# Two up/down layers behind a windowed attention: raw weights loaded in halves, on-chip places handed out by another rule, and q and k of three units loaded first

## The chip, the cores and the metric

The kernel runs on one core of a Trainium2 chip. Its time is the device time of one execution in microseconds (us); 1197.46 us is the median of three runs before the change. The engines are named as in the profile: PE (matrix products; PEld its weight loads), DVE (VectorE), ACT (ScalarE), POOL (GpSimd) and SP (SyncE, which issues all DMAs here).

## What is computed

Windowed attention over 4 batches of 768 positions with 8 heads, then two feed-forward layers over the 3072 tokens, all in float32 out (the weights come in float64):

```
# attention, per chunk of 32 queries: keys are 8 memory slots and positions -16 .. +8 around the chunk
scores = scale * q_c @ k_full.T ; a = softmax(scores) ; out = a @ v_full
x = out, heads joined: [3072, 512]
h = x @ w_in            # [512, 2048]          "up 1"
x = (s * relu(h)**2 + b) @ w_out               # "down 1"
h = x @ w2_in           # [512, 2048]          "up 2"
y = (h - tanh(h)) @ w2_out                     # "down 2"
```

## The kernel before

The program is one stream of code; PE, DVE, ACT and POOL run it in the order in which it is written, and SP issues the DMAs in one queue. Every large product is made of three matmuls on split operands (three(), L132: high by high, low by high, high by low; 128 x 384 results), so each operand is split into a high part by ACT (a copy to the matmul type) and a low part by DVE or POOL (a subtraction).

**Start and up 1** (0 to 398.4 us). Attention runs over 24 units of 128 tokens, three to a block of 384. For a unit u, scores (L192, 16 small matmuls; the masks are added by DVE into sm, L212, and the row maximum taken, L217), exps (ACT), norm (POOL multiplies, L236), transposes (PE, ACT copies into pt), values (PE) and take_x (ACT xh, DVE xl, L276). A block of up 1 has 16 tiles, called slots; a tile needs xh, xl of its three units and wh, wl of a weight pair. The eight pairs (class Pair1, L288) are made from raw float64 words in steps: a (ACT, L145), b (two DVE instructions, L148 and L149), c (DVE, L154), d (ACT, L308), e (DVE, L312); each instruction goes over 1024 columns. Three more sets of eight raw pieces (class Other, L658: w_out, the second w_in, the second w_out) are converted by the same three functions of to_f32 (L138) in the later blocks and stored to HBM. Four tiles make a quad: ob1, ob2 hold its results, POOL combines them into ot1, ot2 (combine1), and five parts are stored to HBM (o<-ob, o<-ot). An agenda of (slot, function) pairs sets when the steps of attention, conversions and loads come between the tiles (L636 to L733).

**Down 1** (to 639.5 us) and **down 2** (from 955.6 us) use a seven-product scheme (P1 to P7) on quadrants, with a ring of split operands (ringh by ACT, ringl by DVE).

**Up 2** (639.5 to 955.6 us) uses seven products as well. It goes in 32 runs, a run being one piece n of weights by one group g of 768 tokens; runs over g 0, 1 come first, those over g 2, 3 behind. In a loop step i (L984) group1(i) makes P1, P6, P5; group3(i - 1) makes P4 and P3 of the run before, adds, applies tanh, lets POOL combine (L337) and stores; group2(i) makes P2 and P7. In every other run the next weights are made by w2_make (ACT w2h, DVE w2l: L802, L803 and L810). In runs 14 to 19 both() (L480) splits x2f, the operands of g 2 and 3, which were put into HBM in down 1.

**Places.** The arena of on-chip memory is cut into places by size in columns of 4 bytes per partition: 3 H (384), 16 G (768), 28 Z (1024), 4 F (1536), 4 E (2048). take() gets one, drop() gives it back with a stamp of the drop counter. grab() (L81) takes, among G and Z that fit, the one dropped longest ago (with an exception that spares Z), else F, else E. A tile in a place can be written only when all readers and writers of the place's last tile are done; that wait lands on the engine that first writes the new tile. The raws (2048 columns) come from E, tmp (three pieces of 384 columns) from F or E, tmp2 (two pieces) from any but H.

Of the kernel before, what the change touches and what calls it, by code (L numbers as in the profile page):

```python
# [25 lines left out]
NB = 384  # L26
# [15 lines left out]
def tile_chunk_attention_two_ffn(  # L42
# [34 lines left out]
    SIZE = {"H": 384, "G": 768, "Z": 1024, "F": 1536, "E": 2048}  # L77
# [3 lines left out]
    clock = [0]  # L81

    def grab(n, only="HGZ"):
        fit = [(free[k][0][0], SIZE[k], k) for k in SIZE if k in only and n <= SIZE[k] and free[k]]
        if any(f[2] in "GZ" for f in fit):
            fit = [f for f in fit if f[2] in "GZ"]
        elif any(f[2] == "F" for f in fit):
            fit = [f for f in fit if f[2] == "F"]
        if not fit and not free["E"]:
            raise MemoryError(sorted((v[1].name.split("_")[0], v[0]) for v in held.values()))  # L90
        if not fit:
            return free["E"].pop(0)[1]
        if n <= SIZE["H"] and free["H"]:
            k = "H"
        else:
            k = min(f for f in fit if f[2] != "Z" or n > SIZE["G"] or len(free["Z"]) > 3 or len(fit) == 1)[2]
        return free[k].pop(0)[1]
# [40 lines left out]
    def to_f32(z, raw):  # L138

        pair = raw.rearrange("p (n two) -> p n two", two=2)  # L140
        lo32, hi32 = pair[:, :, 0], pair[:, :, 1]
        zi = z.bitcast(I32)

        def rebase():
            nc.scalar.activation(out=z, in_=hi32.bitcast(F32), func=AF.Copy, scale=2.0 ** -112)  # L145

        def high():
            nc.vector.tensor_single_scalar(zi, zi, 3, op=ALU.logical_shift_left)  # L148
            nc.vector.scalar_tensor_tensor(  # L149
                out=zi, in0=hi32, scalar=-(1 << 31), in1=zi, op0=ALU.bitwise_and, op1=ALU.bitwise_or  # L150
            )

        def low():
            nc.vector.scalar_tensor_tensor(  # L154
                out=zi, in0=lo32, scalar=29, in1=zi, op0=ALU.logical_shift_right, op1=ALU.bitwise_or
            )

        return rebase, high, low
# [124 lines left out]
    def load_raw(src, n):  # L283
        raw = take(2048, I32, "raw", "E")
        nc.sync.dma_start(out=raw, in_=src.bitcast(I32)[n])
        return raw

    class Pair1:  # L288
# [13 lines left out]
        def c(self):  # L302
            self.low()
            drop(self.raw)
# [182 lines left out]
    def minus(x, y, o=None):  # L487
        o = o if o is not None else take(2 * NB, F32, "t", "GZE")
        nc.gpsimd.tensor_tensor(out=o, in0=x, in1=y, op=ALU.subtract)
        return o  # L490
# [78 lines left out]
    load_qk(0)  # L569
    load_qk(1)  # L570
    load_v(0)
    pairs = [Pair1(0)]
    load_qk(2)
# [3 lines left out]
    load_qk(3)  # L577
    nc.sync.dma_start(out=s_c, in_=s.partition_broadcast(P))
    nc.sync.dma_start(out=b_c, in_=b.partition_broadcast(P))
    pairs.append(Pair1(2))  # L580
    load_v(3)
# [18 lines left out]
    scores(1, (5, 6))  # L600
    exps(0)
# [15 lines left out]
    norm(2)  # L617
    pairs[1].a()
    values(1)
    loads_to(5, 4)  # L620
    take_x(1)
    pairs[1].b()
    transposes(2)
# [3 lines left out]
    values(2)  # L627
    scores(3)
    loads_to(6, 5)
    pairs[1].e(nc.vector)  # L630
    take_x(2)
# [9 lines left out]
    v_slot = {3: 7.0, 4: 10.5, 5: 13.8}  # L641
    for u in range(6, NU):
        v_slot[u] = 16 * (u // 3 - 1) + (3.2, 8.5, 13.6)[u % 3]
    s_slot = {3: 0.0, 4: 3.5}
    for u in range(5, NU):
        s_slot[u] = v_slot[u - 2]
    for u in range(3, NU):
        s0, v0 = s_slot[u], v_slot[u]
        if u > 3:
            at(s0 + 0.001, scores, u)  # L650
        at(s0 + 1.0, exps, u)
        at(s0 + 3.2, norm, u)
        at(v0 - 2.3, transposes, u)
        at(v0, values, u)
        at(v0 + 0.002, take_x, u)
        at(v0 + 0.003, loads_to, u + 4, u + 3)

    class Other:  # L658
# [14 lines left out]
        def c(self):  # L673
            self.low()
            drop(self.raw)
# [119 lines left out]
    def w2_make(n, part):  # L795
        z = z_in[n][part]
        size = (768, 1024)[part]
        h, l = take(size, F32R, "w2h"), take(size, F32R, "w2l")
        if part == 0:
            nc.scalar.activation(out=h[:, 0:512], in_=z[:, 0:512], func=AF.Copy)  # L800
            nc.scalar.activation(out=h[:, 512:768], in_=z[:, 512:768], func=AF.Copy, scale=-1.0)
            nc.vector.tensor_tensor(out=l[:, 0:512], in0=z[:, 0:512], in1=h[:, 0:512].bitcast(F32), op=ALU.subtract)  # L802
            nc.vector.scalar_tensor_tensor(  # L803
                out=l[:, 512:768], in0=z[:, 512:768], scalar=-1.0, in1=h[:, 512:768].bitcast(F32),
                op0=ALU.mult, op1=ALU.subtract,
            )
# [115 lines left out]
    def group1(i):  # L922
        q = quad[i] = {}
        q["a"], q["b"], q["d"] = (bank(k)[:, 0:NB] for k in (i % 2, 2 + i % 3, 5 + i % 3))
        q["tmp"] = take(3 * NB, F32, "tmp", "FE"), take(2 * NB, F32, "tmp2", "GZFE")
        q["p1"], q["u2"], q["u3"] = (q["tmp"][0][:, NB * k:NB * (k + 1)] for k in range(3))
        q["r1"], q["r2"] = (q["tmp"][1][:, NB * k:NB * (k + 1)] for k in range(2))
# [6 lines left out]
    def group2(i):  # L934
# [3 lines left out]
        b1, b2 = (piece(t) for t in q["o"])  # L938
        product(i, "P2", q["a"], False, True)
        product(i, "P7", q["b"], False, True)  # L940
        nc.scalar.activation(out=q["r1"], in_=q["a"], func=AF.Tanh)
        nc.vector.tensor_tensor(out=q["u3"], in0=q["p1"], in1=q["b"], op=ALU.add)  # L942
        nc.vector.tensor_tensor(out=b2[:, 0], in0=q["u3"], in1=q["d"], op=ALU.add)  # L943
        nc.scalar.activation(out=q["r2"], in_=b2[:, 0], func=AF.Tanh)
        nc.vector.tensor_tensor(out=b1[:, 1], in0=q["a"], in1=q["r1"], op=ALU.subtract)
        nc.gpsimd.tensor_tensor(out=b2[:, 0], in0=b2[:, 0], in1=q["r2"], op=ALU.subtract)

    def group3(i):
# [15 lines left out]
        t12, t34 = (piece(t) for t in q["o"][2:])
# [18 lines left out]
    w2_load(1)  # L983
    for i in range(NR + 1):  # L984
# [111 lines left out]
```

## Time and profile before

| | us |
|---|---|
| median of three runs (lowest, highest) | 1197.46 (1196.81, 1198.2) |
| the profiled run | 1198.98 |
| its span, first to last instruction | 1197.2 |
| PE busy in the span | 1093.5 |
| DVE, ACT, POOL busy | 834.9, 569.1, 545.3 |

The profiled run is 1.5 us above the median, and its span 1.8 us below its own time. A row of waits names the line of the waiting instruction, what released it, and the total, the count and the longest of such waits. [...] A tile stands by its name without its number.

### The profile page before, as it was taken

The numbers are of one execution on the slowest core, as the hardware profiler recorded it, in microseconds if no ns is written. First come the engines' busy times: TensorE is split into PE (matmuls) and PEld (weight loads), VectorE is DVE, ScalarE is ACT, GpSimd is POOL, SyncE is SP. The second block draws the span as 40 slices with busy tenths as digits, with TensorE's granted clock in tenths as the row PEclk, the third lists the DMA queues.
The fourth block names the chain that finished last, engine by engine and source line by source line (L and its number), as shares of the span: only waits on it lengthen the run. The fifth ranks groups of instructions, "written<-read, shape, count | busy, mean of one in ns | idle before, by whom it ended". The sixth has DMA issues, their size and how long they took to land. (4 is left out here: it accounts for less than half of the span.)

```text
span 1197.2 us, 19711 instructions
## 1 busy us (share of the span) xinstructions
PE 1093.5 (91%) x7296; PEld 1062.8 (89%) x7296; DVE 834.9 (70%) x1012; ACT 569.1 (48%) x1121; POOL 545.3 (46%) x428
## 2 busy tenths in 40 slices
PE   4789999899999999999899997867897899999998
PEld 3678999899999999999899997856787789999998
DVE  5676777777763776789796776755555596777664
ACT  5455666565653554455453343332233354444442
POOL 2135456689565721324543665533454672231010
PEclk8779999999999999999999999987989899999999
DMA  9965999999988766666475667833545876668783
GB/s 282 296 226 206 351 343 347 363 352 350 349 289 323 263 199 196 195 201 197 161 251 179 239 233 278 284 136 130 194 160 197 324 247 211 187 201 248 235 240 103
DMA packets 129344, 292.28 MB, mean 244 GB/s; under 512 B 10720, under 2 KB 76256, under 8 KB 125152
## 3 DMA queue, kind: packets, MB, share of 16 engines
q1 hardware_dynamic: 129248, 291.02, 71.6%
q8 instruction: 57, 0.93, 0.3%
q14 instruction: 39, 0.32, 0.1%
HBM read 175.38 MB, written 115.61 MB: 243 GB/s over the span
## 5 line engine op out<-in xcount | busy, mean ns | idle before, releaser
L136 PE MATMUL pb<-ringl,whh 128*128 128x384 f32 x896 | 301.4, 336 | 4.1 <-DVE ringl L413 2.4
L134 PE MATMUL pb<-ringh,whh 128*128 128x384 f32 x896 | 300.5, 335 | 3.6 <-ACT ringh L407 3.6
L135 PE MATMUL pb<-ringh,whl 128*128 128x384 f32 x896 | 300.3, 335 | 0.0
L413 DVE TENSOR_TENSOR ringl<-part,ringh 128x768 fp32r<-128x768 f32 x160 | 202.2, 1283 | 79.8 <-ACT ringh L412 79.7
L412 ACT ACTIVATE ringh<-part 128x768 fp32r<-128x768 f32 x160 | 135.0, 848 | 151.7 <-PE pb L135 148.4
L134 PE MATMUL pb<-x2h,w2h 128*128 128x384 f32 x448 | 160.6, 358 | 39.3 <-DVE tmp L942 20.0
L136 PE MATMUL pb<-xl,wh 128*128 128x384 f32 x512 | 175.6, 343 | 6.6 <-DVE xl L276 6.5
L134 PE MATMUL pb<-xh,wh 128*128 128x384 f32 x512 | 179.7, 351 | 0.0
L135 PE MATMUL pb<-xh,wl 128*128 128x384 f32 x512 | 174.9, 342 | 0.0
L136 PEld LDWEIGHTS pb<-ringl,whh 128*128 128x128 f32 x896 | 168.9, 188 | 6.8 <-DVE ringl L413 3.7
L135 PE MATMUL pb<-x2h,w2l 128*128 128x384 f32 x448 | 159.1, 355 | 14.9 <-DVE w2l L810 9.9
L134 PEld LDWEIGHTS pb<-ringh,whh 128*128 128x128 f32 x896 | 169.2, 189 | 3.9 <-ACT ringh L407 3.9
L135 PEld LDWEIGHTS pb<-ringh,whl 128*128 128x128 f32 x896 | 169.0, 189 | 0.0
L136 PE MATMUL pb<-x2l,w2h 128*128 128x384 f32 x448 | 158.1, 353 | 0.0
L329 DVE SCALAR_TENSOR_TENSOR ob<-pb,r 128x384 f32<-128x384 f32 x128 | 69.8, 552 | 91.6 <-ACT r L328 86.2
L134 PEld LDWEIGHTS pb<-x2h,w2h 128*128 128x128 f32 x448 | 90.4, 202 | 47.5 <-DVE tmp L942 22.5
L328 ACT ACTIVATE r<-pb,s_c 128x384 f32<-128x384 f32 x128 | 72.4, 577 | 114.3 <-PE pb L136 108.8
L408 DVE SCALAR_TENSOR_TENSOR ringl<-part,b_c,ringh 128x768 fp32r<-128x768 f32 x64 | 92.6, 1476 | 21.7 <-ACT ringh L407 21.7
L395 POOL TENSOR_TENSOR whl<-s,whh 128x1024 fp32r<-128x1024 f32 x16 | 41.0, 2563 | 144.2 <-ACT whh L394 144.2
L136 PEld LDWEIGHTS pb<-xl,wh 128*128 128x128 f32 x512 | 98.7, 193 | 8.2 <-DVE xl L276 8.1
L135 PEld LDWEIGHTS pb<-x2h,w2l 128*128 128x128 f32 x448 | 90.4, 202 | 17.5 <-DVE w2l L810 11.4
L134 PEld LDWEIGHTS pb<-xh,wh 128*128 128x128 f32 x512 | 99.2, 194 | 2.9 <-issue 0.4
(95 smaller groups left out, 1788.9 us busy)
## 6 DMA issues: line engine op xcount, KB each, us to landing
o<-ot SPq DMA_DIRECT2D x128, 384.0 KB, 4.1
part<-o SPq DMA_DIRECT2D x112, 384.0 KB, 3.9
part<-o SPq DMA_DIRECT2D x56, 768.0 KB, 4.7
o<-ob SPq DMA_DIRECT2D x64, 384.0 KB, 4.5
raw<-in_wi_dram SPq DMA_DIRECT2D x16, 1024.0 KB, 9.3
raw<-in_wo_dram SPq DMA_DIRECT2D x16, 1024.0 KB, 8.1
o<-ob SPq DMA_DIRECT2D x64, 192.0 KB, 3.1
k<-in_qk_dram SPq DMA_DIRECT2D x24, 384.0 KB, 8.6
```

What stands on the lines that cost most here:

```text
L134: nc.tensor.matmul(acc, lhsT=whi, rhs=xhi, start=first, stop=False, skip_group_check=more)
L135: nc.tensor.matmul(acc, lhsT=wlo, rhs=xhi, start=False, stop=False, skip_group_check=more)
L136: nc.tensor.matmul(acc, lhsT=whi, rhs=xlo, start=False, stop=last, skip_group_check=more)
L328: nc.scalar.activation(out=r, in_=ps, func=AF.Identity, scale=s_c[:, 0:1])
L329: nc.vector.scalar_tensor_tensor(out=dst, in0=ps.rearrange("p (n t) -> p n t", n=2), scalar=0.0, in1=r.rearrange("p (n t) -> p n t", n=2), ...
L395: eng.tensor_tensor(out=lo, in0=src, in1=hi.bitcast(F32), op=ALU.subtract)
L408: nc.vector.scalar_tensor_tensor(out=xl, in0=src, scalar=self.bias, in1=xh.bitcast(F32), op0=ALU.add, op1=ALU.subtract)
L412: nc.scalar.activation(out=xh, in_=src, func=AF.Copy)
L413: nc.vector.tensor_tensor(out=xl, in0=src, in1=xh.bitcast(F32), op=ALU.subtract)
```

## The change

Four things are changed.

- **Raw weights in halves.** load_raw takes two tiles of 1024 columns and issues two DMAs; to_f32 goes over 512 results for each half in rebase, high's second instruction and low.
- **Places.** E is gone, its memory becomes eight more Z (36). grab goes through kinds in order: H, then G (from the beginning of up 2 on, when spare is set: the oldest of G, Z and F), then Z, then F. w2h and w2l may use F from then on.
- **tanh into the result's place.** A run of up 2 has one tmp of two pieces of 384 columns in place of tmp and tmp2 with five; each tanh and the sum u3 are written into a half of ob1 or ob2 that is still free. The tanh of P2 and its subtraction come ahead of the two adds of P7.
- **Start.** q and k of units 0, 1 and 2 are loaded first, v behind raw 0; the scores of unit 2 follow those of 1, unit 3's go into the agenda; the slots of units 3 to 5 move by -0.2 to +1.3, those of the later ones by -0.4 to -0.6.

The diff, cut to its core:

```diff
-    COUNT = {"H": 3, "G": 16, "Z": 28, "F": 4, "E": 4}
+    COUNT = {"H": 3, "G": 16, "Z": 36, "F": 4}
     def grab(n, only="HGZ"):
...
+        for kinds in ("H", "GZF" if spare[0] else "G", "Z", "F"):
+            fit = [(free[k][0][0], k) for k in kinds if k in only and n <= SIZE[k] and free[k]]
+            if fit:
+                return free[min(fit)[1]].pop(0)[1]
...
+            for o, lo32, _ in parts:
+                oi = o.bitcast(I32)
+                nc.vector.scalar_tensor_tensor(
+                    out=oi, in0=lo32, scalar=29, in1=oi, op0=ALU.logical_shift_right, op1=ALU.bitwise_or
+                )
...
-        raw = take(2048, I32, "raw", "E")
-        nc.sync.dma_start(out=raw, in_=src.bitcast(I32)[n])
+        raw = [take(1024, I32, nm) for nm in ("raw0", "raw1")]
+        for h in range(2):
+            nc.sync.dma_start(out=raw[h], in_=src.bitcast(I32)[n][:, 1024 * h:1024 * (h + 1)])
...
-        q["tmp"] = take(3 * NB, F32, "tmp", "FE"), take(2 * NB, F32, "tmp2", "GZFE")
+        q["tmp"] = take(2 * NB, F32, "tmp", "GZF")
...
         product(i, "P2", q["a"], False, True)
+        nc.scalar.activation(out=b1[:, 1], in_=q["a"], func=AF.Tanh)
         product(i, "P7", q["b"], False, True)
-        nc.scalar.activation(out=q["r1"], in_=q["a"], func=AF.Tanh)
-        nc.vector.tensor_tensor(out=q["u3"], in0=q["p1"], in1=q["b"], op=ALU.add)
-        nc.vector.tensor_tensor(out=b2[:, 0], in0=q["u3"], in1=q["d"], op=ALU.add)
-        nc.scalar.activation(out=q["r2"], in_=b2[:, 0], func=AF.Tanh)
-        nc.vector.tensor_tensor(out=b1[:, 1], in0=q["a"], in1=q["r1"], op=ALU.subtract)
-        nc.gpsimd.tensor_tensor(out=b2[:, 0], in0=b2[:, 0], in1=q["r2"], op=ALU.subtract)
+        nc.vector.tensor_tensor(out=b1[:, 1], in0=q["a"], in1=b1[:, 1], op=ALU.subtract)
+        nc.vector.tensor_tensor(out=b2[:, 1], in0=q["p1"], in1=q["b"], op=ALU.add)
+        nc.vector.tensor_tensor(out=b2[:, 0], in0=b2[:, 1], in1=q["d"], op=ALU.add)
+        nc.scalar.activation(out=b1[:, 0], in_=b2[:, 0], func=AF.Tanh)
+        nc.gpsimd.tensor_tensor(out=b2[:, 0], in0=b2[:, 0], in1=b1[:, 0], op=ALU.subtract)
...
     w2_load(1)
+    spare[0] = True
```

First place: DVE in up 2, from group2 of one run to group2 of the next, in which weights are made (the names with numbers are the tiles of the two runs). Before:

```order
L931 TENSOR_TENSOR tmp<-tmp,pb 128x384
L954 TENSOR_TENSOR pb<-tmp,pb 128x384
L957 TENSOR_TENSOR pb<-tmp,pb 128x384
L959 TENSOR_TENSOR ob_8267<-pb,tmp_8207 128x384
L960 TENSOR_TENSOR ob_8266<-pb,tmp_8207 128x384
L802 TENSOR_TENSOR w2l<-zina,w2h 128x512
L803 SCALAR_TENSOR_TENSOR w2l<-zina,w2h 128x256
L942 TENSOR_TENSOR tmp<-tmp,pb 128x384
L943 TENSOR_TENSOR ob_8347<-tmp,pb 128x384
L945 TENSOR_TENSOR ob_8346<-pb,tmp_8291 128x384
```

Now:

```order
L929 TENSOR_TENSOR tmp<-tmp,pb 128x384
L952 TENSOR_TENSOR pb<-tmp,pb 128x384
L955 TENSOR_TENSOR pb<-tmp,pb 128x384
L957 TENSOR_TENSOR ob_8407<-pb,ob_8407 128x384
L958 TENSOR_TENSOR ob_8406<-pb,ob_8406 128x384
L801 TENSOR_TENSOR w2l<-zina,w2h 128x512
L802 SCALAR_TENSOR_TENSOR w2l<-zina,w2h 128x256
L940 TENSOR_TENSOR ob_8485<-pb,ob_8485 128x384
L941 TENSOR_TENSOR ob_8486<-tmp,pb 128x384
L942 TENSOR_TENSOR ob_8486<-ob_8486,pb 128x384
```

The subtraction of tanh from P2's bank moves ahead of the two adds of P7, and no row writes a tile of its own for them.

Second place: SP's queue at the beginning of the program. Before:

```order
L183 DMA k<-in_qk_dram 128x768
L184 DMA q<-in_qk_dram 128x512
L183 DMA k<-in_qk_dram 128x768
L184 DMA q<-in_qk_dram 128x512
L188 DMA v<-in_vw_dram 96x1024
L285 DMA raw<-in_wi_dram 128x2048
L183 DMA k<-in_qk_dram 128x768
L184 DMA q<-in_qk_dram 128x512
L188 DMA v<-in_vw_dram 96x1024
L285 DMA raw<-in_wi_dram 128x2048
```

Now:

```order
L181 DMA k<-in_qk_dram 128x768
L182 DMA q<-in_qk_dram 128x512
L181 DMA k<-in_qk_dram 128x768
L182 DMA q<-in_qk_dram 128x512
L181 DMA k<-in_qk_dram 128x768
L182 DMA q<-in_qk_dram 128x512
L284 DMA raw_123<-in_wi_dram 128x1024
L284 DMA raw_124<-in_wi_dram 128x1024
L186 DMA v<-in_vw_dram 96x1024 x2
L284 DMA raw_131<-in_wi_dram 128x1024
L284 DMA raw_132<-in_wi_dram 128x1024
```

The loads of unit 2's k and q move from behind v and raw of the first pair to the third place in front, and each raw is two rows.

Third place: DVE between the first two take_x and the end of the second pair. Before:

```order
L276 TENSOR_TENSOR xl<-pb,xh 128x4x128
L312 TENSOR_TENSOR wl<-z,wh 128x1024
L234 TENSOR_SCALAR sums<-sums 128x8
L235 RECIPROCAL rs<-sums 128x8
L276 TENSOR_TENSOR xl<-pb,xh 128x4x128
L148 TENSOR_SCALAR z<-z 128x1024
L149 SCALAR_TENSOR_TENSOR z<-raw,z 128x1024
L154 SCALAR_TENSOR_TENSOR z<-raw,z 128x1024
L212 TENSOR_TENSOR sm<-pb,mask_mid 128x384 x2
L217 TENSOR_REDUCE nmx<-sm 128x8
L218 TENSOR_SCALAR nmx<-nmx 128x8
L312 TENSOR_TENSOR wl<-z,wh 128x1024
L276 TENSOR_TENSOR xl<-pb,xh 128x4x128
```

Now:

```order
L274 TENSOR_TENSOR xl<-pb,xh 128x4x128
L312 TENSOR_TENSOR wl<-z,wh 128x1024
L274 TENSOR_TENSOR xl<-pb,xh 128x4x128 x2
L142 TENSOR_SCALAR z<-z 128x1024
L145 SCALAR_TENSOR_TENSOR z<-raw_131,z 128x512
L145 SCALAR_TENSOR_TENSOR z<-raw_132,z 128x512
L152 SCALAR_TENSOR_TENSOR z<-raw_131,z 128x512
L152 SCALAR_TENSOR_TENSOR z<-raw_132,z 128x512
L312 TENSOR_TENSOR wl<-z,wh 128x1024
```

The scores of unit 3 (the mask's and the maximum's rows) are no longer among these, and the xl of unit 2 stands right behind that of unit 1, ahead of the second pair's conversion.

## Rows read from the trace of the kernel before

**Rows 1.** Windows by stage: us; busy us (count) of PE, PEld, DVE, ACT, POOL; clock; DMA; GB/s.

```profile
34.20:106.00 71.80, 55.89 (x445) 52.25 (x442) 51.81 (x72) 36.87 (x109) 22.78 (x17) 0.80 0.75 251
106.00:398.40 292.40, 287.35 (x2579) 277.56 (x2578) 206.51 (x302) 166.92 (x460) 188.32 (x163) 1.00 0.91 326
398.40:639.50 241.10, 235.77 (x1344) 234.09 (x1343) 197.19 (x157) 123.77 (x143) 97.61 (x39) 0.99 0.63 207
639.50:730.00 90.50, 87.09 (x494) 84.96 (x493) 65.07 (x107) 36.29 (x74) 54.62 (x53) 1.00 0.66 233
730.00:825.40 95.40, 69.84 (x339) 65.62 (x337) 60.88 (x89) 35.15 (x66) 45.02 (x40) 0.87 0.62 208
825.40:955.60 130.20, 104.92 (x517) 100.54 (x518) 68.75 (x119) 42.28 (x84) 69.12 (x67) 0.88 0.58 208
```

**Rows 2.** PE's waits, 825.4 to 955.6 us: line, releaser, us in total, times, longest.

```profile
PE pb L134 <- DVE tmp L942: 13.0, 6, 2.6
PE pb L134 <- DVE ob L943: 6.5, 4, 4.8
```

**Rows 3.** DVE's waits in the same stretch.

```profile
DVE w2l L802 <- POOL ot L337: 19.2, 6, 3.2
DVE ob L943 <- POOL ot L337: 15.2, 5, 3.8
DVE w2l L810 <- ACT w2h L809: 8.0, 6, 2.6
DVE ob L943 <- DMA o<-ot: 6.5, 3, 5.6
```

**Rows 4.** Timeline of DVE, 888 to 906.5 us: start, duration, instruction, [idle before, releaser].

```profile
895.95 0.56 DVE L943 TENSOR_TENSOR ob<-tmp,pb 128x384 f32<-128x384 f32 x1 [2.79 <-POOL ot L337]
...
903.35 1.46 DVE L802 TENSOR_TENSOR w2l<-zina,w2h 128x512 fp32r<-128x512 f32 x1 [3.20 <-POOL ot L337]
```

**Rows 5.** DVE's waits, 730 to 825.4 us.

```profile
DVE w2l L810 <- POOL ot L337: 4.2, 1, 4.2
DVE ob L943 <- DMA o<-ot: 4.2, 1, 4.2
DVE x2l L484 <- POOL ot L337: 4.1, 2, 3.2
...
DVE x2l L484 <- DMA o<-ot: 1.6, 1, 1.6
```

**Rows 6.** Groups of DVE instructions, 639.5 to 730 us: count, busy us, mean ns, idle before.

```profile
L802 DVE TENSOR_TENSOR w2l<-zina,w2h 128x512 fp32r<-128x512 f32 x6 | 4.2, 693 | 3.0 <-ACT w2h L800 3.0
```

**Rows 7.** DMA issues, 120 to 330 us: count, KB each, median us to landing.

```profile
o<-ot SPq DMA_DIRECT2D x39, 384.0 KB, 7.8
raw<-in_wo_dram SPq DMA_DIRECT2D x11, 1024.0 KB, 8.5
...
zo<-z SPq DMA_DIRECT2D x11, 512.0 KB, 4.4
```

**Rows 8.** PE's waits, 0 to 106 us.

```profile
PE pb L200 <- DMA q<-in_qk_dram: 11.8, 3, 5.1
PE pb L136 <- DVE xl L276: 3.1, 1, 3.1
```

**Rows 9.** Timeline of DVE, 33 to 39 us.

```profile
34.31 1.02 DVE L212 TENSOR_TENSOR sm<-pb,mask_mid 128x384 f32<-128x384 f32 x2 [3.12 <-PE pb L200]
...
36.43 1.22 DVE L312 TENSOR_TENSOR wl<-z,wh 128x1024 fp32r<-128x1024 f32 x1
37.57 0.68 DVE L276 TENSOR_TENSOR xl<-pb,xh 128x512 fp32r<-128x512 f32 x1
```

**Rows 10.** PE's waits, 106 to 398.4 us (up 1, blocks 1 to 7).

```profile
PE pb L136 <- DVE xl L276: 3.4, 2, 2.0
PE pb L259 <- ACT pt L246: 1.5, 2, 1.4
```

**Rows 11.** PE's waits, 398.4 to 639.5 us (down 1).

```profile
PE pb L134 <- ACT ringh L407: 3.6, 1, 3.6
```

More of the change, by code (lines that the diff above doesn't have):

```diff
@@ L73, in tile_chunk_attention_two_ffn @@
     ctx.enter_context(tc.manual_schedule(engines={ET.PE, ET.DVE, ET.Activation, ET.Pool}))
-    SIZE = {"H": 384, "G": 768, "Z": 1024, "F": 1536, "E": 2048}
-    COUNT = {"H": 3, "G": 16, "Z": 28, "F": 4, "E": 4}
+    SIZE = {"H": 384, "G": 768, "Z": 1024, "F": 1536}
+    COUNT = {"H": 3, "G": 16, "Z": 36, "F": 4}
     free = {k: [(0, f"{k}{i}") for i in range(n)] for k, n in COUNT.items()}
     held = {}
-    clock = [0]
+    clock, spare = [0], [False]
     def grab(n, only="HGZ"):
[L84 to L97, printed above, removed]
+        for kinds in ("H", "GZF" if spare[0] else "G", "Z", "F"):
+            fit = [(free[k][0][0], k) for k in kinds if k in only and n <= SIZE[k] and free[k]]
+            if fit:
+                return free[min(fit)[1]].pop(0)[1]
+        raise MemoryError(sorted((v[1].name.split("_")[0], v[0]) for v in held.values()))
     def put_back(place):
@@ L303, in c @@
             self.low()
-            drop(self.raw)
+            for t in self.raw:
+                drop(t)
         def d(self):
@@ L487, in minus @@
     def minus(x, y, o=None):
-        o = o if o is not None else take(2 * NB, F32, "t", "GZE")
+        o = o if o is not None else take(2 * NB, F32, "t")
         nc.gpsimd.tensor_tensor(out=o, in0=x, in1=y, op=ALU.subtract)
@@ L566, in tile_chunk_attention_two_ffn @@
     )
-    load_qk(0)
-    load_qk(1)
+    for u in range(UB):
+        load_qk(u)
+    pairs = [Pair1(0)]
     load_v(0)
-    pairs = [Pair1(0)]
-    load_qk(2)
     load_v(1)
@@ L600, in tile_chunk_attention_two_ffn @@
     scores(1, (5, 6))
+    scores(2, (7, 4))
     exps(0)
@@ L612, in tile_chunk_attention_two_ffn @@
     loads_to(4, 3)
+    norm(2)
     take_x(0)
@@ L621, in tile_chunk_attention_two_ffn @@
     take_x(1)
+    transposes(2)
+    pairs[1].a()
+    values(2)
+    take_x(2)
+    loads_to(6, 5)
     pairs[1].b()
-    transposes(2)
     pairs[1].c()
@@ L639, in at @@
         agenda.append((slot, len(agenda), fn, a_))
-    v_slot = {3: 7.0, 4: 10.5, 5: 13.8}
+    v_slot = {3: 8.3, 4: 11.0, 5: 13.6}
     for u in range(6, NU):
-        v_slot[u] = 16 * (u // 3 - 1) + (3.2, 8.5, 13.6)[u % 3]
-    s_slot = {3: 0.0, 4: 3.5}
-    for u in range(5, NU):
+        v_slot[u] = 16 * (u // 3 - 1) + (2.8, 8.1, 13.0)[u % 3]
+    s_slot = {3: 1.5, 4: 4.0, 5: 6.5}
+    for u in range(6, NU):
         s_slot[u] = v_slot[u - 2]
@@ L674, in c @@
             self.low()
-            drop(self.raw)
+            for t in self.raw:
+                drop(t)
             z = self.z
@@ L797, in w2_make @@
         size = (768, 1024)[part]
-        h, l = take(size, F32R, "w2h"), take(size, F32R, "w2l")
+        only = "GZF" if spare[0] else "GZ"
+        h, l = take(size, F32R, "w2h", only), take(size, F32R, "w2l", only)
         if part == 0:
```

58 lines of the change are left out of this document (25 added, 33 removed).

## The prediction, made before the changed kernel ran

> **What bounds the kernel now.** I read the busy times by stage first [rows 1]. The kernel has one core, TensorE (PE) carries it, and the stages differ: in up 1 after block 0 and in down 1 PE is busy for 98% of the time at full clock (down 2 is the same code as down 1), so nothing that the change does to other engines can be worth much there. The loose time lies in two places. One is block 0 of up 1 with the start ahead of it: PE busy 55.9 us of 71.8, granted clock 0.80. The other is up 2 from 730 us on: PE busy 69.8 of 95.4 and 104.9 of 130.2 us, clock 0.87 and 0.88, while the first twelve of its 32 runs (one run is one piece of the weights by one group of 768 tokens) took 90.5 us with PE busy 87.1 at clock 1.00. The last twelve runs hold as much PE work as the first twelve, so their 130.2 us are 87.1 of matmuls at full clock, 17.8 more because part of them ran at half clock after waits (104.9 - 87.1), and 25.3 of waiting.
>
> Next I asked what PE waits for in those last runs: mostly the DVE adds L942 and L943, which free the banks of the run [rows 2]. What DVE waits for itself is the answer that decides: L802 and L943 stand 19.2 and 15.2 us behind POOL's combine (L337), L943 another 6.5 us behind the store of ot [rows 3]. L802 reads zina and w2h, L943 reads tmp and pb. Neither reads what the combine writes or reads, or what that store reads. So these are waits for a place: w2l and ob were given places that the quad of the run before has just dropped and that POOL or a DMA is still reading. [rows 4] show one such pair: DVE stands 2.79 us at L943 and 3.20 us at L802. In runs 12 to 19 the same stands in four rows, 14.1 us together [rows 5]. By the code, grab prefers G and Z to F by age, keeps E for itself, and the two tmp tiles and four ob/ot tiles of a run turn few places over quickly.
>
> **The change part by part.**
>
> *Places in up 2.* E's four places of 8 KB become eight more Z; tmp shrinks from 3 + 2 pieces to 2, because tanh writes into places of ob; and from up 2 on the oldest free place of G, Z and F is taken. I followed both allocators through the program: before, the takes that DVE waits on get places 2 to 14 drops old; after, every take of up 2 gets one 13 to 28 drops old. A pair of runs drops 16 tiles in its 15.5 us (the first twelve runs are six pairs, 90.5 / 6 = 15.1, and a last one a little longer), so a drop is about 1 us. POOL's four combines take some 4 to 5 us behind the drop. The stores of ot land 7.8 us later even in the saturated stretch of up 1 [rows 7], and sooner, I take it, where DMA is busy 0.6 as here [rows 1]. So 13 drops just cover the worst case, and I take all place waits of up 2 as gone.
> What is late next is PE itself, as in the first twelve runs, which use the same instructions. Runs 20 to 31: 90.5 us, plus some 8 for the end of the last run, whose products wait for their quad and for the first split of down 2, plus 2 for what I can't see: 101, which is -29. Runs 12 to 19 hold 14 splits of x2f (both) on DVE besides: of their 95.4 us the 14.1 of place waits go, and about 3.5 of half clock behind them, so 78, -17.5. Up 2 gives -46.5 by this; the ends are -35, if PE still meets DVE at half of the places, and -57, if both stretches reach the pace of the first twelve.
>
> *Tanh into the result's place.* The operations stay in number. On DVE L945 moves ahead of L942 and L943 (order, first place), so the bank of P7 is added 0.55 us later. In the first twelve runs PE waits 3.4 us in all; it would rise by up to 0.2 us in some runs: +1, ends 0 and +4. POOL's last subtraction comes the same 0.55 us later, with POOL busy 54.6 of 90.5 us [rows 1], and costs nothing.
>
> *Raw weights in halves.* Each of 32 conversions gets two DVE and one ACT instruction more. The price of the split on DVE: 693 ns for 512 columns [rows 6] twice, against 1.22 us for 1024 (L312 in [rows 9]), so some 0.16 us for each extra instruction and 0.32 for a conversion. Eight conversions stand in the start and block 0, +2.6 us on a DVE that sets the pace there; the other 24 stand where DVE is busy 206.5 of 292.4 us [rows 1] and cost nothing; without that cover they would cost 7.7. [...]
> On the queue: in the saturated stretch loads of 1024 KB land after 8.5 us and stores of 512 KB after 4.4 [rows 7], half the bytes in half the time; no gain or loss by size, and 32 more issues on SP. [...]
>
> *Start.* q and k of unit 2 are issued ahead of raw 0 and v (order, second place); scores of 2 follow at once and scores of 3 go into the loop, behind the first tiles. Now PE waits in the start 11.8 us for q loads and 3.1 for xl [rows 8]; the first tile's products stop for 3.1 us because xl of unit 2 stands on DVE behind the scores of unit 3, its maximum and L312: DVE waits 3.12 us for those scores and reaches L276 at 37.57 [rows 9]. After, xl of unit 2 comes in a row with that of unit 1 (order, third place); walking the queue by the rows' durations puts it at about 29.5 us, and the first tile with it: -5 to -8 us for tile 0. But block 0 is paced by DVE (eight conversions of 5 us, masks, results; 51.8 busy of 71.8), which has the same work left. DVE's idle of 3.1 and, I take it, some 5 more that hang on late products go, -8.5; the halves bring +2.6, and the scores of 3, 4, 5 come amid the conversions, with new waits of about 2: -4, ends -10 (tile 0's whole gain stays) and +3 (halves and new waits outweigh).
>
> *Up 1 from 106 us on.* Here G is taken first even if a Z place is older. Two sides. The place wait behind a store in pt (1.5 us on PE) goes, since Z places now lie for over 30 drops, and with it, I take it, the two xl waits of 3.4 [rows 10]: -4.9. Against it sm, q and k now get the places of ot 3.5 slots after their drop, against 5 to 7 before. A slot is 292.4 / 112 = 2.6 us (7 blocks of 16), so 9 us; the store of ot takes 7.8 us (median) [rows 7] behind a combine that itself may lag by 2 to 4. So DVE's mask add or SP's q load will at eleven quads or so stand up to 3 us: DVE has 86 us spare over the seven blocks, PE notices a part: +3, ends 0 and +15. Sum -2.
>
> *Down 1.* One wait of 3.6 us for ringh [rows 11], where ACT stands behind an x2h whose place POOL still reads, and some 1.5 us of half clock after it: -5, ends -6 and 0. Down 2: 0, ends -2 and +2.
>
> **Sum** against the profiled run (span 1197.2, device time 1198.98): -4 - 2 - 5 - 29 - 17.5 + 1 = -56.5, span 1140.7, run 1142.5. The median of the runs is 1197.46, 1.5 below the profiled one: about 1140.
>
> **The rivals.**
> *A. The young G places in up 1 cost more* (15 us instead of 3, or SP's held q load delays stores and raws behind it). For: the stretch moves 326 GB/s and DMA is busy 0.91 [rows 1], landings are long. Against: PE waited only some 5 us there in all. 1150 to 1160.
> *B. Up 2 keeps a chain.* The place waits hide that tmp, combine and store follow each other; L802 then waits for w2h or the zina load and L942 for P7 instead, and half the gain stays. For: DVE also waits 8.0 us for w2h in the last runs [rows 3], which no place explains. Against: the first twelve runs have that chain and run at PE's pace. 1160 to 1175.
> *C. Everything lands:* tile 0's gain stays through block 0, and the last twenty runs take the first twelve's pace. 1112 to 1125.
> *D. Slower.* In up 1 SP's queue is in order. Where a q load must wait for a store of ot that is itself slow in the saturated stretch, every load and store behind waits, those stores hold the next places, and the delay feeds itself. It decides when SP loses over 2 us a quad (28 quads x 2 = 56, the whole gain). Rows 7 against the 9 us above say 0 to 3 us at eleven quads, so it is near but not there. About 1205.
> *E. The places don't come out older,* because the allocator hands them out in another way than I followed. Then only down 1 and the start move: 1188 to 1198.
>
> **How the numbers follow.** Chances: forecast 0.53 (its own range 1128 to 1150), A 0.18, B 0.11, C 0.11, D 0.03, E 0.04. 1140 is that of the likeliest. For 8 in 10 I keep the forecast, A, half of B and most of C: 1115 to 1168. A measurement of this kernel tells about 0.2% (2.4 us) from no change: faster 0.94 (all but D and half of E), same 0.02, slower 0.04.
>
> **What would show it.** Up 2: no DVE wait on POOL L337 at w2l or ob and none on DMA o<-ot, the last two stretches at clock 0.97 or more, the 32 runs in about 271 us (before 316.1). If those waits vanish but PE still idles over 15 us there, B. Start: first full tile near 30 us, block 1 at 100 to 103; if it begins after 106, the DVE walk is wrong. Up 1: waits of DVE's mask add (L210) or SP's q load on o<-ot; over 8 us of PE waits between block 1 and down 1 is A. The prediction fails most likely by the size of the second half of up 2.

## The result and the profile after

The changed kernel takes 1161.68 us (median of four runs, 1159.91 to 1164.49), the kernel before beside it 1197.83 (1196.81 to 1202.14): a ratio of 0.9694, 95% interval 0.9663 to 0.9724. It is faster by 36 us, in the range, where 57 were forecast; the gain is two thirds of what the sum promised. The stages, from the first matmul of each to that of the next, in the two profiled executions:

| us | before | after | moved | forecast |
|---|---|---|---|---|
| start and block 0 | 105.9 | 101.7 | -4.2 | -4 |
| blocks 1 to 7 of up 1 | 292.3 | 295.6 | +3.3 | -2 |
| down 1 | 241.3 | 239.7 | -1.6 | -5 |
| up 2, runs 0 to 11 | 90.5 | 91.5 | +1.0 | +1 |
| runs 12 to 19 | 95.4 | 79.9 | -15.5 | -17.5 |
| runs 20 to 31 | 130.0 | 106.4 | -23.6 | -29 |
| down 2 to the end | 241.8 | 244.9 | +3.1 | 0 |

The windows of the kernel after, by these stages, answer [rows 1] (us; busy us and count of PE, PEld, DVE, ACT, POOL; clock, PE's granted share of its full speed; DMA share; GB/s):

```profile
0.00:101.70 101.70, 70.09 (x689) 62.77 (x690) 74.84 (x113) 56.01 (x174) 27.16 (x42) 0.88 0.90 281
101.70:397.30 295.60, 289.84 (x2578) 277.20 (x2578) 219.02 (x352) 169.48 (x489) 178.66 (x164) 1.00 0.89 321
397.30:637.00 239.70, 234.48 (x1346) 232.82 (x1345) 200.34 (x157) 123.00 (x143) 98.16 (x39) 1.00 0.64 210
637.00:728.50 91.50, 87.84 (x494) 84.83 (x493) 65.74 (x107) 35.91 (x74) 54.85 (x52) 1.00 0.66 229
728.50:808.40 79.90, 65.28 (x338) 61.42 (x336) 62.20 (x90) 34.63 (x66) 47.47 (x40) 0.94 0.68 246
808.40:914.70 106.30, 93.73 (x516) 90.46 (x516) 72.36 (x118) 40.94 (x83) 72.94 (x67) 0.97 0.72 257
914.70:1159.60 244.90, 237.34 (x1344) 235.89 (x1344) 162.16 (x144) 108.41 (x129) 59.12 (x24) 0.98 0.66 207
```

The clock of runs 12 to 31 rose to 0.94 and 0.97, but runs 20 to 31 still leave PE idle for 12.6 of 106.3 us, and in blocks 1 to 7 DVE is busy for 12.5 us more than before ([rows 1]: 206.51). The half clock of the prediction reads so in windows of 1 us of the kernel before: PE stands from 883.9 to 886.4 us, the clock is 0.50 from 886 to 889 us, 0.80 in the next one and 1.00 from 890 us on. DVE's largest waits in up 2, against [rows 3] and [rows 5]:

```profile
DVE tmp L929 <- ACT tmp L927: 19.9, 18, 2.9
DVE w2l L809 <- ACT w2h L808: 10.8, 7, 1.5
...
DVE w2l L809 <- DMA o<-ob: 3.1, 2, 1.5
```

No row names POOL's L337 for w2l, ob or x2l any more: the waits for places are gone, as forecast. Stores stand in 3.1 us, and DVE now waits for ACT's copies instead.

How far can one profile be trusted? Six profiles with the same program up to up 2 (this one and e4, e5, e7, e9, e10 below) begin block 1 between 101.7 and 105.3 us, take 293.0 to 296.6 for blocks 1 to 7 and 239.7 to 241.2 for down 1. So the -4.2 of the start is the best of a spread from -0.6 to -4.2, the +3.3 of blocks 1 to 7 one of a spread from +0.7 to +4.3, and in down 1 next to nothing is shown. In up 2 three profiles with the same operations and rule there (this one, e3, e11) agree within 1.6 us in each stretch. A difference between two single profiles that is not above these spreads shows nothing by itself.

### The profile page after: what moved, and what is told of

Same layout as the page of the kernel before. It is cut to its first block, busy times and chain, and to the rows that moved or that the text cites. A ratio compares the mean times of both kernels' runs of the same rounds, so it can differ in the third digit from the quotient of the medians.

```text
span 1159.6 us, 19768 instructions
## 1 busy us (share of the span) xinstructions
PE 1078.6 (93%) x7296; PEld 1045.4 (90%) x7296; DVE 856.6 (74%) x1076; ACT 568.4 (49%) x1153; POOL 538.4 (46%) x428
## 5 line engine op out<-in xcount | busy, mean ns | idle before, releaser
L413 DVE TENSOR_TENSOR ringl<-part,ringh 128x768 fp32r<-128x768 f32 x160 | 195.9, 1242 | 95.7 <-ACT ringh L412 95.6
L125 PE MATMUL pb<-x2h,w2h 128*128 128x384 f32 x448 | 154.6, 345 | 16.5 <-DVE tmp L929 6.2
L126 PE MATMUL pb<-x2h,w2l 128*128 128x384 f32 x448 | 153.2, 342 | 7.6 <-DVE w2l L809 6.5
L127 PE MATMUL pb<-x2l,w2h 128*128 128x384 f32 x448 | 152.1, 339 | 0.0
L408 DVE SCALAR_TENSOR_TENSOR ringl<-part,b_c,ringh 128x768 fp32r<-128x768 f32 x64 | 94.2, 1500 | 22.1 <-ACT ringh L407 21.8
L125 PEld LDWEIGHTS pb<-x2h,w2h 128*128 128x128 f32 x448 | 85.6, 191 | 23.8 <-DVE tmp L929 9.8
L126 PEld LDWEIGHTS pb<-xh,wl 128*128 128x128 f32 x512 | 97.8, 191 | 0.0
```

Source lines behind the costliest of these rows:

```text
L125: nc.tensor.matmul(acc, lhsT=whi, rhs=xhi, start=first, stop=False, skip_group_check=more)
L126: nc.tensor.matmul(acc, lhsT=wlo, rhs=xhi, start=False, stop=False, skip_group_check=more)
L127: nc.tensor.matmul(acc, lhsT=whi, rhs=xlo, start=False, stop=last, skip_group_check=more)
L408: nc.vector.scalar_tensor_tensor(out=xl, in0=src, scalar=self.bias, in1=xh.bitcast(F32), op0=ALU.add, op1=ALU.subtract)
L413: nc.vector.tensor_tensor(out=xl, in0=src, in1=xh.bitcast(F32), op=ALU.subtract)
```

## The experiments

Each kernel is the changed one but for its edit, where nothing else is said; e1, e2 and so on are their names. Times are medians of four runs; beside them the kernel before took 1199.9 to 1200.7, so 2 to 3 us of a difference to the changed kernel's 1161.68 can come from measuring at another time (the kernel before took 1197.83 there).

**What the age of places is worth in up 2 (e4).** The line that turns the rule over is left out, so G goes first there, and w2h and w2l may not use F:

```diff
-    spare[0] = True
```

> The changed kernel without the switch to the oldest place at up 2: G is taken first there as in up 1, so the tiles of a run get places 0 to 7 drops old while Z places lie idle; the tanh order, the halves, the start are as changed. Theory P (the age of places freed up 2): the last twelve runs go back to 120 us or more (94.7 with the switch, 130.2 before), DVE waits there on POOL L337 and on stores over 30 us in all; the kernel is about as slow as before or slower, 1190 to 1215. Theory T (fewer tiles and the earlier tanh freed up 2): the last twelve runs stay under 100 us, the time within 5 us of the changed kernel.

1254.26 us, ratio to before 1.045 (1.0423 to 1.0477). The three stretches of up 2 take 124.5, 110.1 and 130.1 us. In this code ACT writes first into ob and w2h, so the waits land on ACT, in front of the copies that DVE needs:

```profile
ACT w2h L799 <- POOL ot L337: 48.9, 13, 3.8
...
ACT ob L938 <- POOL ot L337: 42.1, 12, 3.8
```

Theory P holds, with the waits on ACT and not on DVE as I had written, and at a higher price than the 1190 to 1215 us that I had expected. The change without that line would have been 54 us slower than before; more places of 4 KB alone are worth nothing if the youngest are handed out while old ones lie idle.

**What the tanh part does.** Two kernels. e5 has tmp (in F), tmp2 and the order of before, the other places in up 2 taken from G and Z by age. e7, its partner, takes G and Z by age as well and changes nothing else.

```diff
# e5
-        q["tmp"] = take(2 * NB, F32, "tmp", "GZF")
+        q["tmp"] = take(3 * NB, F32, "tmp", "F"), take(2 * NB, F32, "tmp2", "GZ")
# ... and group2, group3 as before; e5 and e7:
-        for kinds in ("H", "GZF" if spare[0] else "G", "Z", "F"):
+        for kinds in ("H", "GZ" if spare[0] else "G", "Z", "F"):
```

> The changed kernel with tmp of three pieces, tmp2 and the old order of tanh in up 2; the oldest place of G and Z is taken there (F only for tmp), ages 10 to 17 drops. Theory P: the last twelve runs take 95 to 99 us, no more than 3 us in DVE waits on POOL L337 or stores. Theory T: they take 110 us or more.

> The changed kernel, but in up 2 the oldest of G and Z is taken, F only where none is free; ages 9 to 16 drops instead of 13 to 28. The F places that down 2's first parts load into have then been free since down 1. If the 6.7 and 2.5 us that PE waits at the beginning of down 2 come from parts whose F place was given to a tile of the last runs, they fall to under 1 us together and the time falls by 6 to 9 us; if the loads are late for another reason they stay. If 9 drops are too young, waits of DVE or POOL on stores of ot come back in the last twelve runs, 5 us or more.

e5 takes 1151.40 us, e7 1162.11, no gain where 6 to 9 us were expected. The 6.9 us that runs 20 to 31 of e7 gained (99.5, see down 2 below) went again in runs 0 to 19 (93.8 and 83.3) and in the start. Not all its places are 9 drops old: by the program, the second half of w2l gets some of 7, and zins some of 2 to 8. At one of these, in run 9, DVE stands 3.3 us behind a store of ob, and runs 9 and 10 take 9.7 and 8.6 us.

In e5 the last twelve runs take 96.8 us, as theory P expects, but DVE's waits for POOL's L337 are 3.6 us there, above the 3 that P allowed. In all of up 2:

```profile
DVE w2l L809 <- POOL ot L337: 9.7, 8, 1.3
```

By the program, the second half of w2l gets a place 7 drops old in three runs, and 9 or more drops in the others. In those three L809 starts some 0.2 us later and takes 2.02 to 2.03 us instead of some 1.26, and they are three of the four runs with new weights outside the stretch of splits (7, 9, 25 and run 1) that take 8.0 to 8.3 us and not 7.3. I read this as 9 drops being enough there and 7 not.

Neither theory had the sign: the old tanh is faster by 10.7 us than its partner, 5.9, 1.8 and 2.7 us of it in the three stretches. So only the order of the operations was tried next (e9), with all tiles as changed:

```diff
+        product(i, "P7", q["b"], False, True)
         nc.scalar.activation(out=b1[:, 1], in_=q["a"], func=AF.Tanh)
-        product(i, "P7", q["b"], False, True)
-        nc.vector.tensor_tensor(out=b1[:, 1], in0=q["a"], in1=b1[:, 1], op=ALU.subtract)
         nc.vector.tensor_tensor(out=b2[:, 1], in0=q["p1"], in1=q["b"], op=ALU.add)
         nc.vector.tensor_tensor(out=b2[:, 0], in0=b2[:, 1], in1=q["d"], op=ALU.add)
         nc.scalar.activation(out=b1[:, 0], in_=b2[:, 0], func=AF.Tanh)
+        nc.vector.tensor_tensor(out=b1[:, 1], in0=q["a"], in1=b1[:, 1], op=ALU.subtract)
```

> The changed kernel, all tiles and places as changed, but in group2 the adds of P7 come first on DVE again and the subtraction of P2's tanh last, and the tanh of P2 stands behind P7 on ACT. Order theory (the subtraction ahead of the adds delays ACT's tanh of that sum, behind it in ACT's queue the copy of the next P1, and so PE by 0.95 us a pair): the first twelve runs take 87 to 89 us instead of 91.5, every run without new weights next to it 7.3, runs 12 to 31 another 4 to 7 us less together, DVE waits on L927 fall; the time falls by 8 to 10 us. Rival (the earlier kernel with tmp of three pieces gained by its tiles or places): 91 us or more, no gain.

1153.54 us; runs 0 to 11 take 86.0 instead of 91.5, runs 20 to 31 101.0 instead of 106.4, and a run with new weights 7.3 instead of 8.2. DVE in such a run of the changed kernel (start, duration, instruction, [idle before, releaser]):

```profile
820.41 1.25 DVE L802 SCALAR_TENSOR_TENSOR w2l<-zina,w2h 128x256 fp32r<-128x256 f32 x1
821.58 0.54 DVE L940 TENSOR_TENSOR ob<-pb,ob 128x384 f32<-128x384 f32 x1
...
822.62 0.55 DVE L942 TENSOR_TENSOR ob<-ob,pb 128x384 f32<-128x384 f32 x1
824.72 1.82 DVE L809 TENSOR_TENSOR w2l<-zins,w2h 128x1024 fp32r<-128x1024 f32 x1 [1.54 <-ACT w2h L808]
826.46 0.54 DVE L929 TENSOR_TENSOR tmp<-tmp,pb 128x384 f32<-128x384 f32 x1
```

ACT's rows beside it:

```profile
823.21 0.53 ACT L943 ACTIVATE ob<-ob 128x384 f32<-128x384 f32 x1 [2.75 <-DVE ob L942]
823.64 1.04 ACT L808 ACTIVATE w2h<-zins 128x1024 fp32r<-128x1024 f32 x1
```

And DVE with the adds first (L941 is the sum b2 there; L802, L809 and L929 are the same):

```profile
818.37 1.24 DVE L802 SCALAR_TENSOR_TENSOR w2l<-zina,w2h 128x256 fp32r<-128x256 f32 x1
...
820.11 0.56 DVE L941 TENSOR_TENSOR ob<-ob,pb 128x384 f32<-128x384 f32 x1
...
822.21 1.31 DVE L809 TENSOR_TENSOR w2l<-zins,w2h 128x1024 fp32r<-128x1024 f32 x1 [1.08 <-ACT w2h L808]
823.44 0.54 DVE L929 TENSOR_TENSOR tmp<-tmp,pb 128x384 f32<-128x384 f32 x1
```

In the first the sum b2 comes behind L940 and ends at 823.2; only then can ACT take its tanh (L943) and, behind it in ACT's queue, the second half of w2h, which L809 waits for, and L929 stands behind L809 with the bank that PE needs. L809 starts 2.10 us behind the sum's start in both. But the sum starts 2.21 us behind L802's start in the first and 1.74 in the second, 0.47 us later, and L809 takes 1.82 instead of 1.31. POOL's subtraction L944 lies beside it in both (the changed kernel, then the other):

```profile
824.45 1.00 POOL L944 TENSOR_TENSOR ob<-ob,ob 128x384 f32<-128x384 f32 x1
```

```profile
822.38 2.01 POOL L944 TENSOR_TENSOR ob<-ob,ob 128x384 f32<-128x384 f32 x1
```

Where POOL began first, DVE's instruction is the long one; where DVE began first, POOL's. The two shares, 0.47 and 0.51, make the 0.95 us or so that PE loses in each pair (8.2 against 7.3 us); this is read from one pair.

**The beginning of down 2 (e7).** PE waits there in the changed kernel:

```profile
PE pb L125 <- ACT ringh L412: 9.2, 2, 6.7
```

and no row of e7 for the beginning of down 2 is over 2 us. SP issues the loads that down 2's first splits read here (changed kernel, then e7):

```profile
894.44 0.37 SPq L844 DMA_DIRECT2D part<-o  x1
...
903.06 0.37 SPq L844 DMA_DIRECT2D part<-o  x1
```

```profile
695.23 0.37 SPq L844 DMA_DIRECT2D part<-o  x1
...
704.91 0.37 SPq L844 DMA_DIRECT2D part<-o  x1
```

With places in F that are free, SP issues them some 200 us ahead. In the changed kernel F is among the oldest places that tiles of the last runs get, so the loads come at the end: that of 903.06 lands at 913.8, and there ACT's split begins and PE goes on. By the program its place had last held a w2l made in run 26, and that of 894.44 an ot. It seems to count who had the place, and not that F is shared: in e5, where F holds tmp to the end, the two loads are issued at 883.71 and 890.29, and down 2 begins 10.3 us behind run 31, as in e7 (17.2 in the changed kernel). Down 2 itself is no shorter in e7 (245.0 us), for PE waits 5.1 us for ringl there.

**What up 1 lost.** Three kernels. e1 has the rule by age from the beginning; e11 has q and k in Z; e2 is the kernel *before* with nothing but the halves, both in the same place of 8 KB:

```diff
# e1
-        for kinds in ("H", "GZF" if spare[0] else "G", "Z", "F"):
+        for kinds in ("H", "GZF" if spare[0] else "GZ", "F"):
# e11
-        qt, kt = take(512, F32, "q", "G"), take(768, F32, "k", "G")
+        qt, kt = take(512, F32, "q", "Z"), take(768, F32, "k", "Z")
# e2, on the kernel before
-        nc.sync.dma_start(out=raw, in_=src.bitcast(I32)[n])
+        for h in range(2):
+            sl = slice(1024 * h, 1024 * (h + 1))
+            nc.sync.dma_start(out=raw[:, sl], in_=src.bitcast(I32)[n][:, sl])
# ... and to_f32 in halves as in the change
```

> Only the rule for places in up 1 differs from the changed kernel: the oldest free place of G and Z is taken, in up 2 as in the change. Theory P (young G places make DVE wait for POOL's combine and for the stores, and PE behind its bank): DVE's waits on POOL ot, on the stores of ot and on loads in blocks 1 to 7 (26 us now) fall under 8, PE's 4.1 us behind L329 fall under 1.5, and the stretch from block 1 to down 1 takes 292 to 293 us instead of 295.7; the time falls by 3 to 4 us. Theory H (the 0.3 us more that DVE spends on each of 24 conversions is what PE meets): the waits on places go, PE still waits about 4 us behind L329, the stretch stays at 295 or more.

> The changed kernel with q and k in Z places instead of G. By the program all tiles of up 1 then get places 15 or more drops old, and no load of q waits in SP's queue for a store of ot. If the young G places cost up 1 its 3.3 us (295.6 against 292.3): SP's waits of L182 on stores (28.7 us) and DVE's waits of L210 on stores (8.8) vanish, the seven blocks take 291 to 293 us, the time falls by 3 to 4 us. Rival (raw halves sharing Z with more tiles come late, as with the rule by age): SP's raw loads wait for places, blocks 4 and 5 take longer, no gain or a loss.

> The kernel before with nothing but the raws cut: two DMAs into the halves of the same 8 KB place and each conversion over 1024 columns in two instructions of 512; places, tanh and start as before. Cost theory: 0.3 us of DVE for each of 32 conversions, met only in block 0, so block 1 begins 2 to 3 us later (about 108.5 instead of 105.9) and the seven blocks behind it keep their 292 us; the time rises by 2 to 3 us. Rival (what up 1 lost in the change comes from the halves and not from the places): the seven blocks take 294 to 296 us with PE waiting for L329, as in the changed kernel.

e1: 1178.59 us, slower by 17. Blocks 4 and 5 take 50.8 and 48.4 us (47.1 and 44.2 in the changed kernel), since raws now get places that stores of ot still read, and the conversions come late (SP, then PE in blocks 1 to 7):

```profile
SPq L284 <- DMA o<-ot: 35.9, 11, 6.6
```

```profile
PE pb L127 <- DVE xl L274: 6.8, 2, 4.5
```

The other 10 us are again the beginning of down 2 (24 us from run 31 to its first matmul, 17 in the changed kernel, and a second wait of 5.3). Neither theory held: G first is right for up 1, because it keeps stores away from the places of the raws.

e11: 1162.29 us, no gain; blocks 1 to 7 take 294.0, inside the spread of the changed program. SP's waits of q loads for stores in the changed kernel are gone,

```profile
SPq L182 <- DMA o<-ot: 28.7, 8, 7.3
```

and nothing followed. So the young G places of the prediction's term do cause waits, but on engines with slack.

e2: 1210.32 us, ratio 1.0077 (1.0057 to 1.0098), slower by 9.6. Block 1 begins at 108.1 (+2.2), and blocks 1 to 7 take 298.6 (+6.3). The rival holds. DVE's conversions in blocks 1 to 7 of e2, and of the kernel before (count, busy us, mean ns):

```profile
L154 DVE SCALAR_TENSOR_TENSOR z<-raw,z 128x512 int32<-128x512 int32 x48 | 47.9, 1038 | 0.8
L161 DVE SCALAR_TENSOR_TENSOR z<-raw,z 128x512 int32<-128x512 int32 x48 | 47.0, 1020 | 0.0
```

```profile
L149 DVE SCALAR_TENSOR_TENSOR z<-raw,z 128x1024 int32<-128x1024 int32 x24 | 38.3, 1597 | 0.8
L154 DVE SCALAR_TENSOR_TENSOR z<-raw,z 128x1024 int32<-128x1024 int32 x24 | 31.1, 1295 | 0.0
```

94.9 us against 69.4: a conversion costs 1.06 us more there, not 0.32. The loads in halves are not the cause: up to down 1 no engine of e2 waits for a raw's load. The timeline tells why: two halves in a row of e2, first with POOL idle, then with POOL at work; then the whole instruction of before with POOL at work:

```profile
172.44 1.29 DVE L154 SCALAR_TENSOR_TENSOR z<-raw,z 128x512 int32<-128x512 int32 x2
...
236.57 2.80 DVE L154 SCALAR_TENSOR_TENSOR z<-raw,z 128x512 int32<-128x512 int32 x2
```

```profile
220.19 1.92 DVE L149 SCALAR_TENSOR_TENSOR z<-raw,z 128x1024 int32<-128x1024 int32 x1
```

Over the trace of e2, 40 of the 64 halves of the first kind ran while POOL was idle, 0.69 us in the mean, 13 for more than nine tenths of their time beside POOL, 1.46; of the whole ones before 1.23 and 1.90. Alone a cut costs 0.15 us, as forecast; beside POOL 1.0.

The same from the other side (e13): the changed kernel with whole raws, whose four places of 8 KB are cut into eight when up 1 is nearly done (a second pool is opened where the first was closed).

> The changed kernel with raws whole again: one load of 1024 KB into a place of 8 KB and conversions over 1024 columns in one instruction, as before; when the last raw is converted (last block of up 1) the four places are cut into the eight of 4 KB that the change has, so that down 1, up 2 and down 2 find the places of the change. Theory of the halves (two halves cost 0.15 us more on DVE alone and 1 to 2 us more beside POOL): block 1 begins 2 us earlier (about 101 to 102 against a middle of 103.8 over the runs of the same code), the seven blocks take 288 to 290 us instead of 293 to 296, up 2 is unchanged within 2 us; the time falls by 6 to 8 us. Rival (the places of up 1 cost the loss): the seven blocks stay at 293 or more.

1150.76 us, 10.9 less, more than the 6 to 8 expected. Blocks 1 to 7 take 287.6, block 1 begins at 97.1 (100.1 and 100.0 in two later kernels with the same code), so the start gave more than I had priced. Whole raws also get places of their own again, and the rest of up 1 has eight Z less; what that does is not tried apart, and it is e2, with all places as before, that shows the cost of the halves. PE's largest wait in blocks 1 to 7, beside the two of the changed kernel:

```profile
PE pb L135 <- DVE ob L330: 0.3, 1, 0.3
```

```profile
PE pb L125 <- DVE ob L329: 4.1, 8, 0.7
PE pb L127 <- DVE xl L274: 1.2, 1, 1.2
```

And in e2, the halves without the other parts, where they came as late xl:

```profile
PE pb L136 <- DVE xl L283: 7.3, 5, 3.5
```

**The start (e3).** The order of loads and first steps and all slots of attention units as before:

> The changed kernel with the order of loads and of the first steps and the slots of the attention units as before. If the start part gave what block 1 gained (it begins at 101.7 instead of 105.9), tile 0 comes at 34 to 37 us again and block 1 begins at 106 to 109 (the halves included); the time rises by 4 to 7 us, the stretches behind keep theirs within 2 us. Rival (the start's order is worth nothing on a block that DVE paces, and the gain comes from places): block 1 still begins before 104.

1174.53 us, 12.9 more. Tile 0 comes at 34.1 again, block 1 at 107.0. I had expected the blocks behind to stay; they take 299.9, 3.3 above the highest of the same program with the new slots. The later units' slots, earlier by 0.4 to 0.6, which I had given no term, are worth some 3 to 5 us: with the old ones PE waits 6.4 us for xl there (1.2 in the changed kernel).

**A better version.** e10: the adds first; no F for tiles of up 2 from run 26 on; weights 7 to 10 made one or two runs earlier. e12: whole raws with that. e15: also 6 of the 14 low parts of x2f on POOL:

```diff
+    made_in = {i: n for i, n in made_in.items() if n not in (7, 8, 9, 10)}
+    made_in.update({11: 7, 13: 8, 15: 9, 18: 10})
...
-    spare[0] = True
+    spare[0] = "GZF"
...
+            if i == 26:
+                spare[0] = "GZ"
# e15 on e12
-            both(op, g, f)
+            both(op, g, f, nc.gpsimd if name in ("P1", "P5", "P3") else nc.vector)
```

> The changed kernel with three things: the adds of P7 ahead of the subtraction of P2's tanh (as in the run on the order); no F place for tiles of up 2 from run 26 on, so that down 2's first loads find F places that have been free for long; weights 7, 8, 9, 10 made one or two runs earlier (in runs 11, 13, 15, 18). Stage by stage: first twelve runs 86 to 88; runs 12 to 19 75 to 77 instead of 79.9 if PE's 12 us of waits for w2h and w2l there come from weights made just before their use (79 or more if the 14 splits on DVE set the pace anyhow); runs 20 to 31 92 to 95 with the wait at the beginning of down 2 under 1 us (101.0 with the order alone); the time 1140 to 1146.

> The last one with whole raws as well. If the parts add up: the gain of the whole raws (6 to 8 us) and of order, tail and weights (15 to 20 us) against the changed kernel, 1134 to 1140 us. If DVE's lateness is shared between them the sum falls short, 1141 or more.

> The last kernel with 6 of the 14 low parts of x2f in runs 14 to 19 made by POOL instead of DVE (those at P1, P5 and P3). If DVE's work sets the pace of runs 12 to 19 (80.9 us there, as against 58 of matmuls), 6 x 1.3 to 1.7 us less of it takes 4 to 7 us off that stretch, to 74 to 77, and PE's waits behind L941 (13 us) fall by as much; the time 1124 to 1127. Rival (DVE pays more for what it does while POOL works, and POOL, busy 54 of 80 us there, then does its combine late): the stretch takes 80 us or more, DVE's instructions beside POOL get longer by what was saved, the time 1130 or more.

e10: 1141.99 us, runs 20 to 31 90.5. Earlier weights gave runs 12 to 19 nothing (80.7): the waits for w2h and w2l went and came back as waits for the adds. Run 20 behind them, though, takes 7.3 us where e9 has 12.5, so that runs 12 to 20 together gain some 3. e12: 1130.19, below the 1134 to 1140 that I had expected, since whole raws take off 11.8 us here and 10.9 in e13: the parts add up. e15: 1125.17, ratio to before 0.9371 (0.9352 to 0.9391), runs 12 to 19 75.4. PE's wait there in e12 and in e15:

```profile
PE pb L135 <- DVE ob L941: 12.0, 5, 4.5
```

```profile
PE pb L135 <- DVE ob L941: 7.6, 4, 3.1
```

So DVE's own work, 14 splits among the adds, sets much of the pace of runs 12 to 19, and POOL had room for some of it.

## Why the prediction was right in direction and too large

- **Forecast and rivals.** 1161.68 lies above the forecast's own 1128 to 1150 and in the band of rival B (a chain is left in up 2, 1160 to 1175), which had 0.11. B's sign is there too: the waits for places vanished, and PE still idles for 27.2 us of runs 12 to 31; the clock in runs 12 to 19 is 0.94 and not 0.97. The chain is the one that e9 and e15 show, tanh, w2h and w2l, and the splits. But B's size is not: up 2 kept 38.1 of the 45.5 us that the sum gave it, not half. Of the 19 us that were missed in the profiled span, 7.4 are in up 2, 5.3 in blocks 1 to 7, 3.4 in down 1 and 3.1 in down 2.
- **Places in up 2** were right as a mechanism: the waits went, and without the rule by age the kernel took 1254 us (e4). The ages that it rests on hold by the program, but for some x2h, x2l and zins at 11 and 12 drops. Runs 12 to 19 came at 79.9 for 78. Runs 20 to 31 missed by 5: 101 had no term for the tanh order in this stretch (5.4, e9), and "some 8 for the end" was nearly right, for there the wait for down 2's loads had taken the place of the one before.
- **Tanh, +1** was the mis-sized term with the longest reach. The 0.55 us were seen, but followed to PE only through the bank of P7, not through ACT's queue: L943, then w2h, then L809, then L929. It cost 5.5 us in runs 0 to 11, where the gain of the places hid it (91.5 net), and 5.4 in runs 20 to 31 (e9); 8.1 us of the median.
- **Halves, +2.6** failed at its step "the other 24 cost nothing": the price came from rows without POOL beside them, and a stage in which DVE is busy for 71% is an average that hides the conversions' bursts ahead of xl and of the banks. They cost 9.6 us on the old kernel (e2) and some 10.9 on the new one (e13, with the raws' places).
- **Young G places, +3,** are not shown to cost anything (e11). What blocks 1 to 7 lost is the halves: three profiles with whole raws take 287.6 to 288.4 us there (e12, e13, e15). The earlier slots gave part of it back (e3). Rival A's stretch was slower than forecast, by another cause.
- **Start, -4** came as -4.2, partly by luck: over the six profiles it is anything from -0.6 to -4.2. The first full tile came at 27.0 us (34.2 before), ahead of the 29.5 of the walk. The new order is worth more (block 1 at 97 to 100 without the halves), and the halves took back some 2 (e2) to 6.
- **Down 1, -5** became -1.6 here and -0.1 to -1.6 over the six profiles. The wait for the place of x2h, which POOL's whl held, is this one in the kernel before:

```profile
595.86 0.84 ACT L483 ACTIVATE x2h<-xr 128x768 fp32r<-128x768 f32 x1 [6.60 <-POOL whl L395]
```

  It went, and DVE and POOL, no longer kept apart by it, met (DVE, then POOL, then PE's waits in down 1 of the changed kernel):

```profile
588.42 5.01 DVE L484 TENSOR_TENSOR x2l<-xr,x2h 128x768 fp32r<-128x768 f32 x2
593.35 3.09 DVE L408 SCALAR_TENSOR_TENSOR ringl<-part,b_c,ringh 128x768 fp32r<-128x768 f32 x1
```

```profile
587.52 5.10 POOL L489 TENSOR_TENSOR xr<-xr 128x768 f32<-128x768 f32 x2 [3.62 <-DVE xr L503]
```

```profile
PE pb L127 <- DVE ringl L408: 4.3, 4, 3.1
```

  Two x2l took 5.01 us beside POOL's 5.10 for two differences; L408 behind them took 3.09, and PE waited 3.1 us, where it had waited 3.6 [rows 11]. With POOL idle an x2l took 0.94 us in the same stretch (at 596.4 us) and L408 1.01 (at 597.2). That DVE's slowness is due to POOL is read from these rows, not tried apart here.
- **Down 2, 0** became +3.1, and the cause is open in part. The term left out that F was now shared with up 2; that cost the 6.9 us ahead of down 2's first matmul, which the table counts with runs 20 to 31, and 2.5 us of waiting behind it. But e7, where the loads come early, takes 245.0 us for down 2 too, with PE waiting 5.1 us for ringl (2.4 before).

## What to carry to other kernels

Where buffers are handed out from a common store, write down beside each take how long ago its place was dropped and who still reads it: a tile waits for the slowest reader of the one before [rows 3], and the oldest place is not always the best, for loads should not inherit the places of stores (in e1 the raws' loads waited 35.9 us for them) or of tiles with late readers (6.7 us of PE's waiting at the beginning of down 2). When an operation is moved ahead on one engine, follow what is queued on the *other* engines behind its result, to the second turn. Price an instruction that is cut in two by rows in which its neighbour engines work as they will work there: here a cut cost 0.15 us with POOL idle and 1.0 beside it.

## What the runs showed of the hardware

In these runs the VectorE (DVE) instructions of the conversions took longer while GpSimd (POOL) worked: the first kind 1.90 us instead of 1.23 over 1024 columns (L149 of the kernel before), but 1.46 instead of 0.69 over 512 (L154 of e2), so that two halves beside POOL cost 1.0 us more than one whole, against 0.15 alone. In the two pairs of L809 and L944 shown above the engine that had begun first took 1.00 us (L944) and 1.31 (L809); where they began second, they took 2.01 and 1.82. In down 1 the end of a wait of 6.60 us on ACT brought DVE and POOL together, and 1.6 of the 5 us expected of it came, as the rows there read.
